# A new order for every instruction of an attention and feed-forward kernel

## The chip, the cores and the metric

One core of one Trainium2 chip runs the whole kernel in one launch. The metric is the time of that launch in device microseconds. Beside it stands a profile of one execution, with a span from the first to the last instruction.

## The reference

Attention with a window of 128 positions and 4 sink positions, then a feed-forward layer with a squared ReLU. q, k and v are 4 x 8 x 768 x 64 in fp32 (batch, heads, positions, head size).

```python
scores = scale * np.matmul(q, k.transpose(0, 1, 3, 2))
keep = is_sink | in_window            # position < 4, or 0 <= query - key < 128
a = softmax(np.where(keep, scores, -1e9))
x = np.matmul(a, v).transpose(0, 2, 1, 3).reshape(3072, 512)
h = x @ w_in                          # 512 x 2048
r = np.maximum(h, 0.0)
out = (r * r) @ w_out                 # 2048 x 512, fp32 out
```

## The kernel before

Matmuls run in bf16 with fp32 accumulation. The four batches pass through the same stages: load, transpose q and k, scores, exp, mask, values, normalize, transpose the result (`xT`), layer 1, ReLU and square (`gT_sb`), layer 2, store. A batch has 6 tiles of 128 positions, worked on in 3 pairs.

Batch 0's q and k come in fp32 by SyncE's queue and are cast ("regroup") and transposed on TensorE. All other q and k tiles, all v tiles and the weights come by DMAs that GpSimd issues, which cast to bf16. Batches 2 and 3 transpose q, k and `xT` with DMA transposes on SyncE's queue. Layer 1 of batches 0 and 1 is plain (`layer1`, L709). Layer 1 of batches 2 and 3 (`layer1_fast`, `quad`, L875) and layer 2 of all but two pairs (`layer2_fast`, L1089) form a product of 2 x 2 blocks from seven smaller products. These need sums of inputs on VectorE (`sum`, L1047: s1 to s4; `xs`), and sums of outputs (`less`, `pair_sum`, `last_quarter`, `middle`).

**What sets the order.** Every piece of work is an `Op` with a number, in the order of its creation, and with the engines that may run it. `Plan.run` walks through the string `ORDER`: the word `57p+60` emits op 57 on TensorE with 60 dummies ahead of it. The letters are p TensorE, v VectorE, a ScalarE (ACT), g GpSimd (POOL), s SyncE's queue. Each engine runs its own ops in that order, and an op waits for the data it reads. So the string decides the order on each engine and, where an op allows more than one engine, also which one runs it. Buffers are handed out in the same walk, so they follow the order too.

On GpSimd, some ops have another form than on VectorE. A mask (`mask 512`) is one multiply by a triangle on VectorE (L587) and two selects on GpSimd (L199). The in-place sums `sum either` (L1047, s3 into `gT_sb`) and `last either` (L1147) are a VectorE add or a DMA from SBUF to SBUF that GpSimd issues and that adds to its destination:

```python
if e == "pool":
    nc.gpsimd.dma_start(out=t_["x"], in_=t_["u"], accum_op=ALU.add)
    return
nc.vector.tensor_tensor(out=t_["x"], in0=t_["x"], in1=t_["u"], op=ALU.add)
```

**Dummies.** `warm` issues transposes of the identity into a tile that is overwritten afterwards. They compute nothing. The last ones of a group are 128 x 128, those ahead of them 32 x 32.

**Ops that the text names** (batch.pair in brackets):

| op | what it is |
|---|---|
| 3, 5, 4 | GpSimd builds the identity, the bias, the triangles |
| 55 k, 56 q; 67 k, 68 q; 61 k, 62 q | regroup of batch 0's head pairs 0; 2; 1 |
| 57 k, 58 q; 69 k, 70 q; 63, 64 | their transposes on TensorE |
| 59 k, 60 q; 71, 72; 65, 66 | unloads of these from PSUM to `qkT` |
| 83, 84; 85, 86 | first scores (with bias), first exps |
| 21, 24, 25, 26; 19, 20, 22, 23 | loads of the four slices of `w_in`; of v |
| 157, 163, 169, ...; 124 | layer 1 of batch 0; transpose of its second pair |
| 257; 259 | a mask of [1.2]; the values that read it |
| 680, 681; 684, 685 | s1, s3 of [2.0]; the products that read them |
| 718, 719; 723 | s1, s3 of [2.2]; the product that reads s3 |
| 830, 831; 835 | the same of [3.0] |
| 691; 693; 694 | a product of [2.0]; its pair sum; its "last either" |
| 664, 666; 672, 674 | masks of [3.2] for the values 668; for 676 |

## Time and profile before

| | |
|---|---|
| time, three runs | 209.57, 211.17, 212.15 us (median 211.17) |
| the profiled execution | 209.85 us, span 208.1 us |
| TensorE (PE) | 199.2 us busy, 96% of the span |
| VectorE (DVE) | 171.5 us, 82% |
| ScalarE (ACT) | 126.4 us, 61% |
| GpSimd (POOL) | 96.1 us, 46% |
| DMA | 26.10 MB in 93882 packets, mean 125 GB/s |

In the profile, L709 is line 709 of the kernel. A row of the waits reads: engine, tile and line that waited, who ended the wait, total in us, times, longest. A group reads: line, engine, operation, output and input with their shape, count, busy us and mean ns of one, then the idle time of the engine just before and what ended it. A piece of the chain that ended last reads: start, length, engine, tile, line, count. A stretch reads: its bounds and length, then busy us and the number of instructions of each engine that touch it, the granted TensorE clock, the mean busy share of the DMA engines, GB/s. PE's matmuls are pipelined and their ends are modelled, so short gaps do not show as idle time.

### The profile page before, as it was taken

How to read it: one execution, taken by the hardware profiler on the slowest of the kernel's cores; microseconds unless marked ns; L12 is line 12 of the kernel's file. 1: busy time of each engine (PE TensorE's matmuls, PEld its weight loads, DVE VectorE, ACT ScalarE, POOL GpSimd, SP SyncE). 2: the span in 40 equal slices, each digit the busy share in tenths (PEclk: the TensorE clock that was granted, in tenths of full speed). 3: DMA queues.
4: the chain of work that ended last, by engine and by line, in shares of the span. 5: the costliest groups of instructions: out<-in, count | busy, mean ns of one | idle time of the engine just before them, and what ended most of it. 6: DMA issues, size and time to landing. Idle time of an engine off the chain costs nothing.

```text
span 208.1 us, 5793 instructions
## 1 busy us (share of the span) xinstructions
PE 199.2 (96%) x2441; PEld 163.7 (79%) x2441; DVE 171.5 (82%) x311; ACT 126.4 (61%) x168; POOL 96.1 (46%) x133
## 2 busy tenths in 40 slices
PE   7788999999999999999999999999999999999993
PEld 6447998568557864568798799999889999999892
DVE  3478669788499782699999999999999889999853
ACT  3594034658988716798774746789964075776110
POOL 7959874399899996480490069400050000000000
PEclk9999999999999999999999999999999999999999
DMA  5999999999999999999914529980024302200025
GB/s 147 283 184 205 179 193 212 172 155 201 160 158 133 158 125 150 137 197 156 241 27 127 79 17 98 93 254 3 0 54 146 58 2 104 102 3 0 0 104 202
DMA packets 93882, 26.10 MB, mean 125 GB/s; under 512 B 86816, under 2 KB 91552, under 8 KB 93856
## 3 DMA queue, kind: packets, MB, share of 16 engines
q0 software_dynamic: 69248, 12.59, 79.1%
q1 hardware_dynamic: 24280, 12.94, 28.9%
q8 instruction: 19, 0.31, 0.7%
q10 hardware_dynamic: 328, 0.20, 0.3%
q14 instruction: 7, 0.06, 0.1%
HBM read 27.30 MB, written 6.29 MB: 161 GB/s over the span
## 4 chain that ended last, share of the span: by engine, by line
PE 73%; POOL 10%; DMA 5%; ACT 3%; DVE 3%; issue 3%; ACTq 0%; SPq 0%
PE py L1089 26%; PE pm L875 18%; PE pm L709 17%; PE po L634 4%; POOL v L343 4%; POOL qn L332 4%; PE ps L555 4%; DMA qn<-in_k_dram 4%; POOL expm L199 2%; PE py L970 2%; ACT expm L575 2%; DMA qr<-in_q_dram 2%; PE po L609 1%; PE pt L445 1%; ACT qs L180 1%
## 5 line engine op out<-in xcount | busy, mean ns | idle before, releaser
L575 ACT ACTIVATE expm<-ps 128x1024 bf16<-128x1024 f32 (+1 forms) x48 | 44.3, 955 | 5.9 <-PE ps L555 5.8
L709 PE MATMUL pm<-xT,w_in_sb 128*128 128x256 bf16 (+1 forms) x320 | 44.0, 294 | 0.4 <-ACT r L720 0.4
L199 POOL TENSOR_SCALAR_AFFINE_SELECT expm<-expm 128x512 bf16<-128x512 bf16 x32 | 24.3, 793 | 42.7 <-ACT expm L575 42.6
L709 PEld LDWEIGHTS <-w_in_sb 128*128 128x128 bf16 x320 | 34.5, 114 | 6.9 <-issue 0.6
L1089 PEld LDWEIGHTS <-gT_sb 128*128 128x128 bf16 x336 | 31.1, 98 | 3.7 <-issue 0.2
L1089 PEld LDWEIGHTS <-sg 128*128 128x128 bf16 x240 | 22.4, 98 | 3.3 <-issue 0.6
L720 ACT ACTIVATE r<-pm 128x1024 bf16<-128x1024 f32 x14 | 14.3, 1025 | 17.3 <-PE pm L709 17.1
L875 PE MATMUL pm<-xs,w_in_sb 128*128 128x128 bf16 (+1 forms) x256 | 24.0, 246 | 0.0
L343 POOL DMA_DIRECT2D v<-in_v_dram x24 | 21.4, 899 | 2.6 <-DMA qn<-in_q_dram 1.6
L875 PEld LDWEIGHTS <-w_in_sb 128*128 128x128 bf16 x256 | 22.1, 114 | 0.2
L332 POOL DMA_DIRECT2D qn<-in_q_dram x20 | 17.7, 887 | 8.8 <-DMA w_out_sb<-in_moe_w_out_dram 5.9
L897 ACT ACTIVATE gT_sb<-r 128x1024 bf16<-128x1024 bf16 x19 | 19.5, 1053 | 2.4 <-DVE r L949 2.3
L1089 PE MATMUL py<-wt,gT_sb 128*128 128x256 bf16 x160 | 20.8, 273 | 0.0
L1089 PE MATMUL py<-wt,sg 128*128 128x256 bf16 x160 | 20.6, 273 | 0.0
L332 POOL DMA_DIRECT2D qn<-in_k_dram x20 | 17.7, 890 | 2.3 <-issue 1.1
L1089 PE MATMUL py<-w_out_sb,gT_sb 128*128 128x256 bf16 x144 | 18.5, 273 | 0.0
L650 DVE TENSOR_TENSOR xn_sb<-po,rc 128x512 bf16<-128x512 f32 (+1 forms) x28 | 17.2, 615 | 1.0
L937 ACT ACTIVATE r<-pm 128x1024 bf16<-128x1024 f32 x11 | 11.2, 1024 | 10.2 <-DVE sg L1047 5.8
L722 DVE TENSOR_SCALAR r<-pm 128x1024 bf16<-128x1024 f32 x10 | 12.1, 1228 | 5.7 <-PE pm L709 5.7
L875 PEld LDWEIGHTS <-qkT 128*128 128x128 bf16 x192 | 16.1, 114 | 0.5 <-issue 0.4
L922 DVE TENSOR_TENSOR t<-t,pm 128x512 f32<-128x512 f32 x24 | 15.5, 681 | 1.0 <-ACT t L180 0.5
L949 DVE CUSTOM_DVE_ANT_1 r<-pm,t 128x1024 bf16<-128x1024 f32 x12 | 14.4, 1220 | 1.8 <-PE pm L875 1.4
(95 smaller groups left out, 324.4 us busy)
## 6 DMA issues: line engine op xcount, KB each, us to landing
out_dram<-osb SPq DMA_DIRECT2D x11, 512.0 KB, 3.9
v<-in_v_dram POOLq DMA_DIRECT2D x24, 128.0 KB, 7.8
qn<-in_k_dram POOLq DMA_DIRECT2D x20, 128.0 KB, 8.3
qn<-in_q_dram POOLq DMA_DIRECT2D x20, 128.0 KB, 7.8
w_in_sb<-in_moe_w_in_dram POOLq DMA_DIRECT2D x4, 512.0 KB, 10.8
w_out_sb<-in_moe_w_out_dram POOLq DMA_DIRECT2D x4, 512.0 KB, 11.1
qr<-in_k_dram SPq DMA_DIRECT2D x4, 256.0 KB, 5.0
qr<-in_q_dram SPq DMA_DIRECT2D x4, 256.0 KB, 6.0
```

The lines of the kernel that those rows point to most:

```text
L199: nc.gpsimd.affine_select(out=e_tile, in_=e_tile, compare_op=ALU.is_ge, fill=fill, base=i - 1, pattern=[[0, n], [1 if i else -1, 128]], ch ...
L332: nc.gpsimd.dma_start(out=qn_t[b, ti][:, t, :].rearrange("p (h d) -> p h d", d=D), in_=(q, k)[ti][b, :, 128 * t:128 * t + 128, :].rearrang ...
L343: nc.gpsimd.dma_start(out=v_sb[b % 2][:, t, :, 0:D], in_=v[b, :, 128 * t:128 * t + 128, :].rearrange("h p d -> p h d"))
L575: nc.scalar.activation(out=x[:, :, o:512], in_=bank_t["s", b, s, m][:, :, o:512], func=AF.Exp, scale=scale)
L650: touch(("po", b, s, m0), e, nc.vector.tensor_tensor(out=xn_sb[:, 2 * s:2 * s + 2, :].rearrange("p i (j q h d) -> q p j i h d", j=2, q=2, ...
L709: nc.tensor.matmul(pm[:, i, :], lhsT=w_in_sb[:, fb // 4, kb, fb % 4:512:4], rhs=xT[:, c0 // 256:(c0 + cw) // 256, kb, :], start=(kb == 0), ...
L720: nc.scalar.activation(out=o, in_=h, func=AF.Relu)
L875: touch(tag, e, nc.tensor.matmul(y[:, bk, :, i, :], lhsT=weights(name, f0 + i, a), rhs=rhs[:, a, :], start=fresh and i == 0 and a == 0, st ...
L897: nc.scalar.activation(out=d, in_=x, func=AF.Square)
L922: touch(tag, e, nc.vector.tensor_tensor(out=T["t"], in0=T["t"], in1=bank(bk), op=ALU.subtract), bk)
L949: touch(tag, e, nc.vector._custom_dve(TENSOR_ADD_SAT, out=r, in0=both(), in1=t, s0=3.4028235e38, s1=0.0), 0, 1)
L1089: ins = nc.tensor.matmul(y_, lhsT=x[:, i, :], rhs=r_, start=(first or tail and n == 2) and i == 0, stop=i == HB - 1, skip_group_check=not ...
```

## The change

The string `ORDER` is replaced as a whole, with the same 888 ops, and one constant of `warm`. Here are the lines around the ops that the text names; every other line of the string changes too.

```diff
 ORDER = """
-0v 8s 9s 1v 56a 55a 3g 7a 10s 57p+60 58p 60v 11s 5g 6g 19g 4g 20g 67v 69p+12 21g 68g 59a 12s 13s 70p+1 83p 71a 61v
-72a 14s 15s 22g 23g 84p 63p 102p 65v 85a 62a 86a 24g 25g 79g 103p 106a 73v 74v 64p 75p 76p 104a 66v 91p 113p 78v 93a
...
-635p 685p 687p 638a 636a 686v 578v 662p 626p 639v 565v 683v 637v 688p 690v 579v 561a 663a 640p 575a 689a 641v 665a
...
+0v 5g 3g 8s 9s 4g 55a 10s 11s 12s 1v 19g 13s 14s 15s 57p+47 59a 67v 7a 69p+21 56a 58p 60a 71a 68v 70p+1 61a 83p 72v
+62a 85a 84p 86a 63p 103p 102p 64p 73v 75p 20g 21g 65v 74v 6g 22g 23g 24g 25g 104a 66v 106a 91p 76p 105v 78v 87p 89p
...
+550v 574a 575a 589a 590p 591p 684p 576p 577p 611g 453g 491g 654g 592v 635p 622s 623s 457s 656g 638a 682v 686v 495s
+681g 685p 636a 551a 687p 683v 578v 624g 637v 690v 621s 639v 689v 593v 662p 626p 688p 663a 640p 691p 642s 579v
...
+675p 667p 649p 705a 737a 701v 674g 666g 668p 694g 669v 738v 650p 651v 707p 672g 709v 676p 677v 756p 742p 744a 743p
...
         for i in range(P.dummies):
-            n = 32 if P.dummies - i > 24 else 128
+            n = 32 if P.dummies - i > 18 else 128
```

What follows from the two strings:

- Dummies: 60 + 12 + 1 before, of which 36 are small; 47 + 21 + 1 after, of which 29 + 3 are small. Each group ends with its full ones: 24 before, 18 after at most.
- GpSimd starts with the bias (5) and the identity (3) comes second; before it was the other way round. A regroup (68) leaves GpSimd.
- ACT takes 55, 59, 56, 60, 71, 61, 62 ahead of the first exp (85); before, 56, 55, 59, 71, 72.
- 58p stands behind 69p and its dummies; before, it stood ahead of them.
- VectorE to GpSimd: seven "last either" (453, 472, 491, 694, 713, 732, 844) and three "sum either" (681, 719, 831), all of which are accumulating DMAs there, and 8 masks. GpSimd to VectorE: 5 masks and the regroup.
- Between ACT and VectorE: to VectorE go 6 ReLUs, 8 squares, 4 unloads and 1 strided one, 3 transposed copies, 8 copies, 4 "first_quarter", 2 "first", 1 evacuation; to ACT go 5 ReLUs, 11 squares, 5 unloads and 1 strided one, 3 transposed copies, 3 copies, 1 "first_quarter" and 1 regroup.
- TensorE has the same steps in another order; the 28 steps ahead of 157 are the same set.

More of the change, by code (lines that the diff above doesn't have):

```diff
@@ L18 @@
 ORDER = """
-0v 8s 9s 1v 56a 55a 3g 7a 10s 57p+60 58p 60v 11s 5g 6g 19g 4g 20g 67v 69p+12 21g 68g 59a 12s 13s 70p+1 83p 71a 61v
-72a 14s 15s 22g 23g 84p 63p 102p 65v 85a 62a 86a 24g 25g 79g 103p 106a 73v 74v 64p 75p 76p 104a 66v 91p 113p 78v 93a
-87p 77a 115a 89p 88v 105v 80v 90v 95p 92p 94a 26g 116g 81p 107g 96v 114p 82a 97p 119p 27g 28g 29g 30g 31g 32g 33g
-108p 98v 117a 99p 109p 100a 118v 120p 111p 122p 101v 157p 121v 112v 123v 110v 163p 124p 169p 164v 126v 16s 125v 166p
-170v 160p 161a 158v 167v 175p 176v 168v 2v 131p 133a 162a 127g 128p 178p 179v 130v 129v 132v 34g 35g 36g 37g 38g 39g
@@ L24 @@
-40g 41g 180v 172p 173a 287p 137p 145p 136p 42g 43g 44g 45g 147a 177v 148v 288p 140a 289p 134p 146p 174v 141v 138a
-139v 159v 290p 46g 47g 48g 49g 50g 291p 149a 150v 135a 151p 142p 143p 144v 152p 292p 153v 293p 154p 155v 156a 294p
-165a 295v 171a 296a 181p 272v 184p 182a 196p 199p 202p 185a 187p 205v 201v 183a 200a 204v 273v 190p 197v 274v 203a
-188a 189v 198a 216p 191a 217a 276p 277p 297s 234p 219a 51g 52g 53g 54g 353g 220v 235a 193p 194a 278p 218v 186v 195v
-206v 279p 237a 226p 229a 354g 355g 356g 357g 358g 359g 360g 361g 280p 209p 372s 275v 210a 212a 227a 192v 298v 299v
@@ L29 @@
-362g 363g 364g 365g 374s 371s 375s 373s 281p 282p 284a 221p 248p 245p 211v 213v 222v 247a 249a 283p 285a 302p 377s
-376s 366g 246v 250v 207p 367g 261p 208a 262a 238v 236v 214p 230v 215v 303p 305p 228g 304a 264a 253p 239p 300v 254a
-256a 368g 240p 241v 306p 223p 263g 369g 231p 251p 301v 370g 232p 224a 225a 252a 594g 265g 257g 595g 596g 233v 307a
-308v 309p 258p 266p 242p 597g 311v 244v 255v 310p 378s 380s 17s 243a 312v 313p 259p 267p 335p 260v 314v 315a 387p
-268v 329p 388a 330a 338p 336v 390a 339a 340v 331v 326p 394p 317p 327a 598g 599g 600g 397a 269p 318v 271a 328a 270v
@@ L34 @@
-395a 320p 411p 321a 412a 332p 333a 414a 398v 384v 391v 396v 389v 413v 322v 323p 392p 399p 324a 319a 334a 337v 393v
-400v 325v 341p 379s 403p 347p 342v 381s 612s 614s 601g 316s 382s 458v 404a 460v 459v 439v 350p 348a 406a 421p 616s
-613s 462p 424a 602g 603g 604g 605g 383g 464a 422a 463p 465p 385p 415g 351v 440v 349v 407v 461v 423g 352a 386a 466p
-416p 429p 417p 432a 405v 468v 615s 402s 617s 619s 286s 441v 430a 418v 496v 467v 469p 425g 433g 431g 344p 401s 501v
-18s 426p 408p 618s 409p 427p 471v 345a 470p 473p 428v 472v 410v 474v 504v 443p 444p 628p 346a 445a 475a 498v 505v
@@ L39 @@
-434p 446p 629a 448a 631a 442v 502v 497v 435p 447p 652p 420s 476s 449v 450p 419s 630v 436v 438s 437s 451p 500v 625v
-454p 655a 343a 477v 644p 653a 506p 647a 507p 520p 521p 508a 510p 645a 522a 481p 452v 503v 478v 453v 479v 482p 509v
-523v 499v 480v 511v 524p 484p 525v 512p 526p 513p 455v 486a 483a 514a 527p 632v 528a 485p 646g 516p 517p 530p 606g
-537v 534v 488p 456a 529a 535v 518v 536v 487v 531p 633p 580p 490v 532v 489p 491v 634v 581p 582a 492p 493v 552p 566p
-567p 583v 533a 515a 584p 553p 494v 538p 586p 539p 607g 654g 621s 620s 495s 608g 622s 457s 568a 519a 609g 623s 610g
@@ L44 @@
-611g 648v 624g 585v 680v 540a 554a 541v 587p 542p 556p 588a 555v 589a 543v 544p 557v 569v 656g 590p 545p 570p 546a
-558p 559p 591p 682v 560a 547a 571v 681v 592v 572p 548p 549p 573p 574a 593a 562p 563p 550v 551a 684p 564v 576p 577p
-635p 685p 687p 638a 636a 686v 578v 662p 626p 639v 565v 683v 637v 688p 690v 579v 561a 663a 640p 575a 689a 641v 665a
-691p 627a 692p 670p 671a 718v 657p 699v 666v 642s 693v 672g 695p 658p 673a 664g 700v 703p 694v 659v 696v 643s 704p
-705a 697a 706p 649p 675p 667p 650p 674v 701v 651v 676p 668p 737a 738v 669v 707p 742p 743p 756p 744a 746p 757p 758a
@@ L49 @@
-708a 740v 677v 760p 722p 698s 660s 741v 719v 723p 739v 702v 710p 759v 745v 761v 747v 709v 661s 748p 749p 762p 711p
-678s 763p 764a 765a 714p 725p 727a 724a 679s 750v 720v 752p 766p 753p 751a 712v 713v 721v 715v 716a 770v 726p 767p
-729p 754v 728v 768v 717s 816p 817p 730p 771v 731v 732v 774p 772v 773v 733p 769a 818a 819v 734v 775p 802p 820p 803p
-776a 777v 804a 806p 735a 805v 821v 788p 778p 822p 755a 790a 807v 823p 830v 824a 789p 808p 792p 809p 826p 827p 779v
-832v 780p 810a 812p 781p 813p 791v 831v 794p 793v 828v 795p 782a 796a 834p 797a 829a 833v 783v 835p 784p 811v 814v
@@ L54 @@
-785p 786v 798p 799p 836a 837p 736s 825a 815a 800v 838p 840v 839v 801v 841p 787a 843v 849v 842p 868v 845p 850v 853p
-854p 856p 855a 851v 857p 872p 869v 873p 870v 875p 858v 844v 846v 859v 847a 852v 860p 848s 861p 864p 862v 871v 863v
-865v 877a 874a 878v 866v 876p 879p 881v 882v 867s 880p 883p 887s 884v 886s 885v
+0v 5g 3g 8s 9s 4g 55a 10s 11s 12s 1v 19g 13s 14s 15s 57p+47 59a 67v 7a 69p+21 56a 58p 60a 71a 68v 70p+1 61a 83p 72v
+62a 85a 84p 86a 63p 103p 102p 64p 73v 75p 20g 21g 65v 74v 6g 22g 23g 24g 25g 104a 66v 106a 91p 76p 105v 78v 87p 89p
@@ new lines @@
+93a 113p 26g 79g 77a 107g 95p 92p 115a 90v 116g 80v 88v 94a 114p 96v 81p 82a 97p 27g 98v 119p 108p 99p 117a 118v
+109p 100a 101v 111p 120p 122p 28g 29g 30g 31g 32g 33g 34g 35g 123v 121v 110v 112v 157p 163p 124p 164v 126v 169p 125a
+158v 160p 166p 161a 167v 170a 175p 128p 131p 178p 129a 133a 159v 162v 176v 172p 179v 287p 130v 132v 168v 145p 173a
+36g 37g 127g 38g 39g 40g 41g 177a 165v 2v 42g 174v 180v 136p 137p 147a 140a 148v 138a 139v 141v 288p 289p 134p 290p
+146p 43g 291p 44g 45g 46g 135a 142p 149a 150v 151p 143p 152p 292p 144v 293p 153v 154p 295v 156a 47g 48g 49g 294p 50g
@@ new lines @@
+296a 51g 52g 53g 155v 184p 272v 54g 353g 181p 16s 185v 205v 199p 196p 202p 171a 182a 190p 201a 200a 187p 186v 197a
+371s 297s 198v 203v 204a 191v 273v 354g 355g 356g 188a 216p 192v 217a 274v 276p 277p 193p 194v 357g 358g 359g 360g
+361g 362g 219a 17s 195v 189a 234p 235a 237a 278p 279p 226p 280p 227a 238g 209p 220v 183v 298v 210a 218v 374s 212a
+281p 299v 228v 363g 229a 230g 372s 375s 364g 236g 221p 282p 248p 245p 283p 378s 377s 206v 300v 222v 246v 302p 211v
+247v 373s 249a 250a 284v 285a 207p 213v 208a 261p 264a 303p 304a 262a 214p 275v 305p 307a 215v 253p 254a 265g 239p
@@ new lines @@
+365g 383g 255g 366g 367g 368g 256a 240p 263v 241v 369g 306p 301v 223p 379s 376s 231p 251p 225v 232p 224a 309p 252a
+233v 370g 594g 595g 308v 258p 266p 242p 244a 310p 243v 267p 311v 257v 268v 313p 259p 335p 314v 260v 315a 387p 336a
+329p 390a 388a 394p 395a 317p 338p 397a 326p 389v 312v 391v 318v 319a 339a 330v 596g 396v 269p 597g 398v 327v 271v
+320p 411p 270a 340a 331a 321v 414a 412a 322a 328a 598g 599g 600g 384v 415v 332p 333v 612s 382s 381s 316s 392p 323p
+601g 602g 413g 603g 604g 605g 399p 324a 393v 334v 400v 341p 337a 325a 403p 380s 18s 406a 616s 402s 347p 404a 458v
@@ new lines @@
+348a 342a 460v 405v 459v 462p 350p 421p 351a 422a 424a 463p 385p 423g 425g 407g 465p 439v 461v 441v 464v 625v 466p
+386a 416p 429p 467a 614s 432a 440v 617s 613s 442v 401s 606g 607g 286s 615s 417p 469p 497v 418v 344p 408p 352a 430a
+431g 433g 426p 409p 427p 343a 345a 619s 608g 468v 471v 496v 470p 473p 443p 618s 501v 444p 428v 609g 472g 434p 474v
+410v 445v 499v 475a 349a 628p 620s 629a 446p 631a 435p 502v 498v 652p 447p 505v 450p 448v 653a 449v 436v 452v 451p
+346a 644p 655a 454p 645a 647a 520p 506p 521p 507p 508a 510p 500v 503v 477v 455v 478v 419s 479v 509v 511v 522v 438s
@@ new lines @@
+476s 437s 481p 482p 420s 484p 483v 504v 512p 513p 523v 524p 514a 487v 526p 485p 525v 480v 456v 536v 486a 630v 516p
+527p 528a 632v 517p 518v 534v 488p 530p 490v 531p 537v 532v 633p 634v 580p 489p 492p 582a 529a 538p 493v 540a 494v
+581p 539p 583v 535v 552p 553p 584p 566p 567p 542p 515a 554a 568a 555v 541v 543v 556p 558p 544p 545p 557v 559p 570p
+569v 572p 586p 585v 587p 533a 519a 546a 560a 680v 571v 562p 563p 548p 547a 588a 648v 564v 561a 549p 573p 610g 646g
+550v 574a 575a 589a 590p 591p 684p 576p 577p 611g 453g 491g 654g 592v 635p 622s 623s 457s 656g 638a 682v 686v 495s
@@ new lines @@
+681g 685p 636a 551a 687p 683v 578v 624g 637v 690v 621s 639v 689v 593v 662p 626p 688p 663a 640p 641v 691p 642s 579v
+692p 565a 665a 627a 670p 657p 658p 673a 671a 695p 693v 699v 643s 718v 703p 664v 700v 659v 704p 719g 696v 697v 706p
+675p 667p 649p 705a 737a 701v 674g 666g 668p 694g 669v 738v 650p 651v 707p 672g 709v 676p 677v 756p 742p 744a 743p
+702v 757p 746p 741v 740v 739v 745v 708a 758a 722p 723p 748p 760p 660s 759v 747v 710p 749p 762p 711p 712v 761v 763p
+764a 750a 698s 679s 714p 720v 725p 661s 766p 767p 678s 772v 724v 715v 726p 752p 753p 721v 729p 728v 768v 770v 716a
@@ new lines @@
+765a 754v 816p 774p 751v 818v 727a 775p 817p 731v 730p 733p 755a 776a 777v 819v 771v 820p 802p 734v 735v 769a 830v
+778p 803p 804a 805v 788p 790a 789p 822p 780p 821v 806p 792p 823p 713g 831g 824a 791v 807v 773v 808p 809p 794p 779v
+826p 827p 810a 825v 793v 828v 812p 781p 795p 813p 832v 796a 782a 732g 717s 834p 736s 797a 829a 811a 833v 814v 835p
+836v 798p 799p 784p 783a 785p 837p 800v 838p 786v 841p 840v 839a 801v 787v 842p 845p 815a 843v 849v 853p 868v 850v
+872p 851v 846v 869v 855a 844g 854p 856p 873p 852v 847v 857p 875p 858a 859v 870v 848s 874a 860p 861p 864p 876p 862v
@@ L57 @@
+877v 878v 863v 871v 879p 880p 865v 866a 881v 882v 867s 884v 883p 887s 886s 885v
 """
```

## Prediction

> **What bounds the kernel now.** I read the page first (two lines), then the busy time of each engine in long stretches (two rows).

> ```profile
> span 208.1 us, 5793 instructions
> PE 199.2 (96%) x2441; PEld 163.7 (79%) x2441; DVE 171.5 (82%) x311; ACT 126.4 (61%) x168; POOL 96.1 (46%) x133
> ...
> 0.00:19.10 19.10, 14.48 (x236) 10.50 (x237) 10.94 (x31) 12.65 (x18) 15.38 (x32) 1.00 1.21 205
> 19.10:203.00 183.90, 182.94 (x2189) 151.72 (x2186) 158.55 (x276) 113.74 (x150) 80.76 (x102) 1.00 1.09 115
> ```

> The columns after the length are PE, weight loads, DVE, ACT, POOL. From 19.1 us, where the first layer-1 product starts, to 203.0, PE is idle for 183.90 - 182.94 = 0.96 us. Its waits there are few (the waits of PE in that stretch, then the end of the chain of waits, then one line of the DMA issues):

> ```profile
> PE po L634 <- POOL expm L199: 0.4, 1, 0.4
> PE pm L709 <- ACT r L720: 0.4, 1, 0.4
> PE pm L875 <- ACT expm L575: 0.2, 1, 0.2
> ...
> 198.60 4.38 PE py L1089 x40
> 203.00 0.43 DVE u L1120
> 204.77 0.29 DVE half L182
> ...
> out_dram<-osb SPq DMA_DIRECT2D x1, 64.0 KB, 2.0
> ```

> Three waits, 1.0 us. The rest of the span is the front (19.1 us, PE idle for 4.6 of it and on dummies for several more) and the tail: four VectorE instructions behind the last sums, a store that lands 2.0 us after its issue. So the kernel is bound by TensorE's own work behind a front that its feeders set. A new order has the same matmuls (4 dummies fewer), so it can win only the front, 1.0 us of waits and the tail. That bound carries the forecast.

> **The front.** The 28 TensorE steps ahead of the first layer-1 product (157p) are the same set in both orders, and the layer-1 products behind it begin 157, 163, 124, 169 in both; what moves is when 157p starts. Timeline rows of the start, then one group of the identity tile, then two stretches with that tile alone:

> ```profile
> 1.15 0.29 POOL L225 TENSOR_SCALAR_AFFINE_SELECT ident<-ident 128x128 bf16<-128x128 bf16 x1 [0.63 <-DVE ident L207]
> 1.42 0.77 POOL L199 TENSOR_SCALAR_AFFINE_SELECT biases<-biases 128x256 bf16<-128x256 bf16 x2
> 1.50 3.81 PE L173 MATMUL pt<-ident 32*32 32x32 bf16 x60 [1.50 <-POOL ident L225]
> 2.92 0.30 POOL L236 MEMSET biases<- 4x256 bf16 x1
> 4.58 0.63 ACT L180 ACTIVATE qs<-qr 128x512 bf16<-128x512 f32 x1 [2.48 <-DMA qr<-in_q_dram]
> 8.56 1.08 ACT L180 ACTIVATE qkT<-pt 128x512 bf16<-128x512 bf16 x2 [1.55 <-PE pt L445]
> 9.53 0.82 ACT L575 ACTIVATE expm<-ps 128x768 bf16<-128x768 f32 x1
> 16.83 1.02 ACT L575 ACTIVATE expm<-ps 128x1024 bf16<-128x1024 f32 x1 [0.27 <-PE ps L555]
> ...
> L173 PE MATMUL pt<-ident x73: 182/219/311, 1.5 to 8.4; 128*128 128x128 bf16 x37, 32*32 32x32 bf16 x36
> ...
> 3.00:4.00 1.00, 1.00 (x12) 1.00 (x11) 0.00 (x0) 0.00 (x0) 1.00 0.97 338
> 6.45:7.05 0.60, 0.60 (x15) 0.60 (x12) 0.00 (x0) 0.00 (x0) 1.00 1.02 352
> ```

> *The identity is late.* GpSimd now builds the bias (5g) before the identity (3g), and every dummy reads the identity. The bias ends at 2.92 + 0.30 = 3.22, the identity 0.29 later, so the dummies start at about 3.6 instead of 1.50.

> *The clock.* The last two rows count dummies that touch a stretch: 12 in 1.0 us with a length of 0.31 (the largest of L173) is one each 0.107 us; 15 in 0.6 us with 0.22 (the median) is one each 0.056. So TensorE ran at half rate up to about 6.3, although the granted clock reads 1.00, which only says that nothing was recorded earlier. The 60 dummies: (3.81 - 0.31 - 24 x 0.107) / 36 = 0.026 us for a small one.

> *The new dummies.* 29 small and 18 full: 0.75 + 1.93 us, from 3.6 to 6.3, which is when 57p's four real transposes begin (about 5.8 before). With 0.43 for them and 0.2 of latency, the first unload (59a) starts at 6.9.

> *ACT's list.* 60a unloads the q transposes (58p), which now stand behind 69p with its 21 dummies: from 6.7, 3 x 0.026 + 18 x 0.056 to 0.107, then eight transposes and the latency, so 60a starts at 8.45 if the clock opens at once, at 9.75 if it does not. Then 60, 71, 61 and 62 pass ACT at 0.5 each (two unloads between 8.56 and 9.53), and the first exp starts at 10.4 to 11.8 instead of 9.53. From there to the end of the eighth exp ACT took 17.85 - 9.53 = 8.3 us, of which 0.5 was 62a, now done: 7.8, so it ends at 18.2 to 19.6 instead of 17.85, and 157p behind it moves by +0.35 to +1.75. ACT's waits for PE in that list (0.27 in the row) may shrink. I take **+0.7**.

> On the other side, an early front is stopped by the weights (a timeline row, the landing of `w_in_sb`'s four loads, a piece of the chain):

> ```profile
> 9.49 1.51 POOL L279 DMA_DIRECT2D w_in_sb<-in_moe_w_in_dram  x2
> ...
> DMA to landing us min/median/max: 9.2/10.8/11.9
> ...
> 23.13 7.11 PE pm L709 x64
> ```

> 169p reads the third slice, issued at about 10.2; it lands by 10.2 + 11.9 = 22.1 and 169p starts at 23.1. GpSimd reaches that issue at 9.9 in the new order (0.6 of regroup gone from it, nothing else ahead that was not there), so 157p gains at most about 1.3.

> [...]

> **What moves from VectorE to GpSimd.** Ten in-place sums become accumulating DMAs that GpSimd issues: seven "last either" (L1147) and three "sum either" (L1047). None ran in before. Three more masks go to GpSimd on balance. Groups by line and shape, then DMA issues (the first between 120 and 140 us, the others of the whole run):

> ```profile
> L1147 DVE TENSOR_TENSOR osb<-osb,u 128x256 f32<-128x256 f32 x10 | 5.1, 512 | 0.1
> L1047 DVE TENSOR_TENSOR gT_sb<-gT_sb 128x1024 bf16<-128x1024 bf16 x10 | 6.8, 684 | 0.0
> L199 POOL TENSOR_SCALAR_AFFINE_SELECT expm<-expm 128x512 bf16<-128x512 bf16 x32 | 24.3, 793 | 42.7 <-ACT expm L575 42.6
> L332 POOL DMA_DIRECT2D qn<-in_k_dram x20 | 17.7, 890 | 2.3 <-issue 1.1 <-DMA v<-in_v_dram 0.5 <-DMA qn<-in_q_dram 0.4
> ...
> qn<-in_k_dram POOLq DMA_DIRECT2D x2, 128.0 KB, 3.6
> ...
> qn<-in_k_dram POOLq DMA_DIRECT2D x20, 128.0 KB, 8.3
> w_out_sb<-in_moe_w_out_dram POOLq DMA_DIRECT2D x4, 512.0 KB, 11.1
> ```

> VectorE loses 7 x 0.51 + 3 x 0.68 = 5.6 us by this. That is worth nothing by itself: PE waits for VectorE nowhere after 19.1 by the rows above. What it costs is latency. An issue holds GpSimd for 0.89 us and lands after 3.6 us when the queues are quiet (loads at 122 to 126 us) and after as much as 11.1 when they are full. Which end counts is read from who waits. A "last either" is waited for by a store alone. A "sum either" feeds a matmul. I place these by PE's own work, in steps like these pieces of the chain:

> ```profile
> 143.49 0.87 PE py L1089 x8
> 144.36 0.87 PE pm L875 x8
> 145.24 0.43 PE ps L555 x8
> 149.38 0.36 PE po L634 x12
> ```

> 681g can start when 680v has read its source, about when PE is at 140; 685p needs it, and nine quad products of four matmuls (0.44 each), 684p (0.87) and a score (0.43) lie between: 5.3 us. For 719g before 723p it is about 8 us, for 831g before 835p about 9. After 100 us the load queue is thin (loads of batch 3 alone), so I take the quiet 3.6 us, or 5 for twice the bytes: **0**, with no cover left at 681g. At 11.1 the waits are 5.8, 3.1 and 2.1: **+11**.

> **One new wait that can be added up.** GpSimd's queue near 152 us reads 719g, 674g, 666g, 694g, 672g. 719g waits for the sum 718v, which stands behind 693v, which waits for the product 691p. So three masks are queued behind an accumulation. From the end of 691p: 0.2 latency, VectorE 0.4 + 2 x 0.7 = 1.8, then GpSimd 0.89 + 2 x 1.59 + 0.89 + 1.59 = 6.55: 8.5 us. On PE from there to 676p, which reads the last mask, there are six sums (5.2), scores and values: 8.0 us. **+0.5**; between 0, if VectorE runs ahead, and more by as much as it runs late.

> **Waits that go.** The longest wait after 19.1 (values 259p for a mask on GpSimd, at 75 us) goes, since that mask (257) is on VectorE again: **-0.4**; of the other 0.6 I count nothing, and all 1.0 as the bound. The tail has the same last steps: 0.

> **Sum.** +0.7 - 0.4 + 0.5 = +0.8 on the profiled execution's 209.85 us (span 208.1 and 1.75 around it): 210.65. The median shown, 211.17, is 1.32 above that execution, so I forecast **212.0**. The best end is -1.3 - 1.0 = -2.3, or 208.9.

> **Rivals.**
> *A sum that lands late* (slower). The three accumulations before matmuls land with the latency of a full queue. For it: no row shows this DMA, it reads two operands, and 681g has 5.3 us. Against: the queue is nearly empty then, and 3.6 us is measured there. It decides from 5.3 us on; at 8.3 us (the page's median for k loads) it costs 3.0 + 0.3 = 3.3, at 11.1 it costs 11: 215.3 to 223, middle 219. Chance 0.22.
> *VectorE late, and masks behind it* (slower). VectorE is busy 158.55 of the middle's 183.9 us, and two-input multiplies on it meet GpSimd's masks (timeline rows):

> ```profile
> 63.71 2.88 DVE L587 TENSOR_TENSOR expm<-expm,tri 128x1024 bf16<-128x1024 bf16 x3
> ...
> 65.38 1.70 POOL L199 TENSOR_SCALAR_AFFINE_SELECT expm<-expm 128x512 bf16<-128x512 bf16 x2
> ```

> Three multiplies take 2.88 us, and a mask beside them 1.70 against 1.59. If VectorE is 3.5 us behind near 150 us, 676p waits 4 us: 216. The 5.6 us taken off VectorE speak against it, its other moves (two "first", five copies, a relu more) give some 2 back. Chance 0.18, 0.14 of it beyond 2%.
> [...]
> *A late clock.* [...] Chance 0.12, within 2%.
> *The gains alone.* The front finds its 1.3 us and no new wait opens: 208.9. For it: ACT's 0.27 us waits and PE's 4.6 idle us in the front. Chance 0.10; 0.05 more for something the trace does not show that gains over 2%.

> **How the numbers follow.** Forecast 0.33, late clock 0.12, gains 0.10 and the milder part of the VectorE case 0.04 stay within 2%: 0.59, less 0.02 for the forecast's own upper tail, 0.57. Slower by over 2%: 0.22 + 0.14 + 0.02 = 0.38. Faster by over 2%: 0.05, because 4.2 us aren't there to be won. Two per cent is about what a measurement of this kernel can tell from no change. The likeliest case alone spans 209.0 to 214; to leave out no more than 2 in 10, the range goes from 209.0 into the late sums, to 218.0.

> **What would show it.** First dummy at about 3.6 us; full-rate dummies not before 7; first exp at 10.4 to 11.8; first L709 product at 19.5 to 20.9; PE idle from there to the end under 2 us, with a wait of some 0.5 us for GpSimd near 158; accumulations landing within 5 us. Wrong, if 157p starts before 18, if PE waits for a sum's DMA near 145, 162 or 185, or if VectorE releases PE over and over between 100 and 190.

## The result, and the profile after

The new order takes 211.19 us (median of 22 runs, 210.79 to 211.44) against 209.83 us for the order before (22 runs on the same chip, 209.45 to 212.15). The ratio is 1.0059, 95% interval 1.0047 to 1.0072: a small loss, far inside two per cent. The profiled execution took 211.43 us, with a span of 209.7. In experiments 1, 2 and 3 below, two, one and two of the twelve runs lay over 1.5% above the fastest; the ratios leave them out, the medians do not.

The page and the two long stretches of after, to be laid beside those of before (columns after the length: PE, weight loads, DVE, ACT, POOL, granted clock, DMA share, GB/s):

```profile
span 209.7 us, 5812 instructions
...
PE 199.6 (95%) x2432; PEld 164.2 (78%) x2437; DVE 167.9 (80%) x306; ACT 124.3 (59%) x161; POOL 105.6 (50%) x148
...
0.00:19.10 19.10, 14.19 (x185) 10.46 (x185) 8.91 (x27) 12.20 (x18) 14.40 (x30) 1.00 1.21 208
19.10:203.00 183.90, 182.11 (x2212) 150.87 (x2217) 156.32 (x274) 111.68 (x143) 91.19 (x119) 1.00 1.24 124
```

The work moved off VectorE (171.5 to 167.9 us) to GpSimd (96.1 to 105.6), and TensorE is as full as it was. The span grew by 1.6 us, and the timeline rows of the start show where (of before the first layer-1 product, then the rows of after):

```profile
19.14 3.11 PE L709 MATMUL pm<-xT,w_in_sb 128*128 128x256 bf16 x27
...
3.52 2.98 PE L173 MATMUL pt<-ident 32*32 32x32 bf16 x47 [3.52 <-POOL ident L225]
6.30 0.63 PE L445 MATMUL pt<-ident,qs 128*128 128x128 bf16 x4
6.86 2.29 PE L173 MATMUL pt<-ident 32*32 32x32 bf16 x21
8.94 1.06 PE L445 MATMUL pt<-ident,qs 128*128 128x128 bf16 x8
20.77 1.47 PE L709 MATMUL pm<-xT,w_in_sb 128*128 128x256 bf16 x12
...
3.88 0.63 ACT L180 ACTIVATE qs<-qr 128x512 bf16<-128x512 f32 x1 [1.78 <-DMA qr<-in_k_dram]
6.97 0.60 ACT L180 ACTIVATE qkT<-pt 128x512 bf16<-128x512 bf16 x1 [2.46 <-PE pt L445]
6.97 1.28 ACTq L363 DMA_DIRECT2D vs_in<-in_v_dram  x1
8.30 0.63 ACT L180 ACTIVATE qs<-qr 128x512 bf16<-128x512 f32 x1 [0.74 <-issue]
10.04 1.09 ACT L180 ACTIVATE qkT<-pt 128x512 bf16<-128x512 bf16 x2 [1.11 <-PE pt L445]
12.05 4.08 ACT L575 ACTIVATE expm<-ps 128x768 bf16<-128x768 f32 x5
```

The first dummy waits for the identity until 3.52. The first cast is done at 3.88 + 0.63 = 4.5, but 57p's four transposes stand behind 47 dummies and start at 6.3. ACT unloads them at 6.97, then issues the load of `vs_in` (the row of that issue runs to 8.25; ACT's idle 0.74 us fall almost wholly into it), then casts q (56a) at 8.30. TensorE's eight transposes of 69p and 58p at 8.94 still run at half rate (1.06 us; four take 0.40 at full rate, at 8.13 in before). So 60a starts at 10.04, the first exp at 12.05 (9.53 before) and the first layer-1 product at 20.77 (19.14 before): +1.63. From there to the end of the span it is 209.7 - 20.8 = 188.9 us, and 208.1 - 19.1 = 189.0 before. **In these two executions the whole difference is the front.**

Waits of PE from 20.8 us on, and the piece of the chain around the longest:

```profile
PE po L634 <- POOL expm L199: 0.6, 2, 0.3
PE pm L709 <- ACT r L720: 0.4, 1, 0.4
PE py L970 <- issue: 0.3, 2, 0.2
...
155.03 2.83 POOL expm L199 x4
157.86 0.81 POOL osb L1145
158.67 1.25 POOL expm L199 x2
159.97 0.63 PE po L634 x15
```

The chain spells out the queue that the prediction added up: masks, the accumulation 694g, the mask 672g, then 676p. The wait at 75 us is gone. In place of 1.0 us of waits there are 1.3, and the same matmuls were busy for some 0.5 us less.

The new accumulating DMAs (KB each, then the median time from issue to landing):

```profile
osb<-u POOLq DMA_DIRECT2D x7, 128.0 KB, 3.3
gT_sb<-gT_sb POOLq DMA_DIRECT2D x3, 256.0 KB, 3.9
```

### The profile page after: what moved, and what is told of

Read it like the earlier page. It is cut to its first block, busy times and chain, and to the rows that moved or that the text cites. A ratio compares the mean times of both kernels' runs of the same rounds, so it can differ in the third digit from the quotient of the medians.

```text
span 209.7 us, 5812 instructions
## 1 busy us (share of the span) xinstructions
PE 199.6 (95%) x2432; PEld 164.2 (78%) x2437; DVE 167.9 (80%) x306; ACT 124.3 (59%) x161; POOL 105.6 (50%) x148
## 4 chain that ended last, share of the span: by engine, by line
PE 82%; ACT 6%; DVE 5%; POOL 3%; issue 2%; POOLq 0%; DVEq 0%; ACTq 0%
PE py L1089 24%; PE pm L709 20%; PE pm L875 16%; PE py L970 7%; PE po L634 4%; PE ps L555 4%; ACT expm L575 3%; PE pt L173 2%; POOL expm L199 2%; ACT gT_sb L897 1%; PE px L679 1%; DVE sg L1047 1%; PE po L609 1%; ACT qkT L180 1%; PE pt L426 1%
## 5 line engine op out<-in xcount | busy, mean ns | idle before, releaser
L575 ACT ACTIVATE expm<-ps 128x1024 bf16<-128x1024 f32 (+1 forms) x48 | 43.5, 953 | 3.1 <-PE ps L555 2.9
L709 PE MATMUL pm<-xT,w_in_sb 128*128 128x256 bf16 (+1 forms) x320 | 44.4, 294 | 0.4 <-ACT r L720 0.4
L709 PEld LDWEIGHTS <-w_in_sb 128*128 128x128 bf16 x320 | 34.3, 114 | 6.8 <-issue 1.0
L199 POOL TENSOR_SCALAR_AFFINE_SELECT expm<-expm 128x512 bf16<-128x512 bf16 x38 | 26.7, 766 | 18.6 <-ACT expm L575 18.4
L1089 PEld LDWEIGHTS <-gT_sb 128*128 128x128 bf16 x336 | 30.8, 98 | 4.2 <-issue 1.0
L1089 PEld LDWEIGHTS <-sg 128*128 128x128 bf16 x240 | 22.6, 98 | 3.0 <-issue 0.4
L875 PE MATMUL pm<-xs,w_in_sb 128*128 128x128 bf16 (+1 forms) x256 | 23.6, 246 | 0.0
L343 POOL DMA_DIRECT2D v<-in_v_dram x24 | 22.3, 936 | 1.3 <-DMA qn<-in_q_dram 1.0
L875 PEld LDWEIGHTS <-w_in_sb 128*128 128x128 bf16 x256 | 22.1, 114 | 0.1
L937 ACT ACTIVATE r<-pm 128x1024 bf16<-128x1024 f32 x12 | 11.9, 1023 | 15.1 <-PE pm L875 13.4
L332 POOL DMA_DIRECT2D qn<-in_q_dram x20 | 17.8, 898 | 6.1 <-DMA w_out_sb<-in_moe_w_out_dram 4.4
L1089 PE MATMUL py<-wt,gT_sb 128*128 128x256 bf16 x160 | 20.8, 273 | 0.0
L722 DVE TENSOR_SCALAR r<-pm 128x1024 bf16<-128x1024 f32 x12 | 14.6, 1221 | 7.6 <-PE pm L709 7.6
L1089 PE MATMUL py<-wt,sg 128*128 128x256 bf16 x160 | 20.6, 273 | 0.0
L1145 POOL DMA_DIRECT2D osb<-u x7 | 6.6, 945 | 27.7 <-DVE u L1120 27.7
L897 ACT ACTIVATE gT_sb<-r 128x1024 bf16<-128x1024 bf16 x18 | 18.5, 1055 | 2.3 <-DVE r L949 2.3
L720 ACT ACTIVATE r<-pm 128x1024 bf16<-128x1024 f32 x12 | 12.1, 1023 | 11.4 <-PE pm L709 11.4
L332 POOL DMA_DIRECT2D qn<-in_k_dram x20 | 17.8, 898 | 1.5 <-issue 0.9
L1089 PE MATMUL py<-w_out_sb,gT_sb 128*128 128x256 bf16 x144 | 18.5, 273 | 0.0
L1045 POOL DMA_DIRECT2D gT_sb<-gT_sb x3 | 2.6, 868 | 28.5 <-PE pm L875 11.4
## 6 DMA issues: line engine op xcount, KB each, us to landing
out_dram<-osb SPq DMA_DIRECT2D x11, 512.0 KB, 3.1
v<-in_v_dram POOLq DMA_DIRECT2D x24, 128.0 KB, 8.1
qn<-in_k_dram POOLq DMA_DIRECT2D x20, 128.0 KB, 7.1
qn<-in_q_dram POOLq DMA_DIRECT2D x20, 128.0 KB, 7.6
w_in_sb<-in_moe_w_in_dram POOLq DMA_DIRECT2D x4, 512.0 KB, 11.2
w_out_sb<-in_moe_w_out_dram POOLq DMA_DIRECT2D x4, 512.0 KB, 10.4
```

The costliest lines, as they stand in the source:

```text
L199: nc.gpsimd.affine_select(out=e_tile, in_=e_tile, compare_op=ALU.is_ge, fill=fill, base=i - 1, pattern=[[0, n], [1 if i else -1, 128]], ch ...
L332: nc.gpsimd.dma_start(out=qn_t[b, ti][:, t, :].rearrange("p (h d) -> p h d", d=D), in_=(q, k)[ti][b, :, 128 * t:128 * t + 128, :].rearrang ...
L343: nc.gpsimd.dma_start(out=v_sb[b % 2][:, t, :, 0:D], in_=v[b, :, 128 * t:128 * t + 128, :].rearrange("h p d -> p h d"))
L575: nc.scalar.activation(out=x[:, :, o:512], in_=bank_t["s", b, s, m][:, :, o:512], func=AF.Exp, scale=scale)
L709: nc.tensor.matmul(pm[:, i, :], lhsT=w_in_sb[:, fb // 4, kb, fb % 4:512:4], rhs=xT[:, c0 // 256:(c0 + cw) // 256, kb, :], start=(kb == 0), ...
L722: nc.vector.tensor_scalar_max(o, h, 0.0)
```

## The experiments

Ratios are to the order before, run beside each kernel on the same chip, with their 95% intervals. All edits are to the order of after, unless said otherwise.

**1. The identity first.**
```
-0v 5g 3g 8s 9s
+0v 3g 5g 8s 9s
```

> Edit: in the order of after, the identity (3g) is built ahead of the bias (5g); nothing else moves. Theory (the late identity makes the front): first dummy at about 1.5 us instead of 3.52; its 47 dummies (2.7 us) end before the first cast (55a, 3.88 to 4.5), so 57p's transposes start at 4.5 to 4.6 instead of 6.30; the full rate comes near 6.3; the unload of the q transposes (60a) starts at 7.6 to 8.2 instead of 10.04 and the first L709 product at 18.3 to 19.0 instead of 20.77. Time 208.7 to 209.6, 1.6 to 2.5 under after. Rival (ACT's casts and the queued loads set the front, not the identity): the first L709 product moves by less than 0.5 us, time 210.7 to 211.3.

Measured: 210.64 us, ratio 1.0028 (1.0000 to 1.0056). Its timeline:

```profile
1.50 2.98 PE L173 MATMUL pt<-ident 32*32 32x32 bf16 x47 [1.50 <-POOL ident L225]
7.23 1.04 PE L445 MATMUL pt<-ident,qs 128*128 128x128 bf16 x8
19.35 2.89 PE L709 MATMUL pm<-xT,w_in_sb 128*128 128x256 bf16 x25
```

The late identity is worth 1.42 us of the front's 1.63 in this pair of profiles. The place of the first product moves from execution to execution (20.12 to 20.78 in five with the front of after, 19.35 here and 19.41 in experiment 12, which has this front), so 0.7 to 1.4 is what these rows support. The ratios give 0.31%, some 0.65 us; this kernel's runs spread from 209.75 to 212.13. The expectation was too hopeful by 0.4 us at the first product, and the time is 1 us above its range: TensorE ran from 1.50 on and its transposes at 7.23 were still at half rate (1.04 us for eight). The full rate did not come at 6.3 as in before.

**2. No dummies ahead of 57p.**
```
-57p+47
+57p
```

> Edit: in the order of after, the 47 dummies ahead of the first transposes (57p) are left out; the 21 ahead of the q transposes stay. Theory A (the dummies stand in the way: 57p waits for their end, 1.9 us behind its data): 57p at 4.6, the first unload at 5.0, ACT's second cast at about 6.4, 60a at 8.2 instead of 10.04, and what the later clock takes back is under 1 us: time 209.6 to 210.4. [...]

Measured: 210.11 us, ratio 1.0004 (0.9978 to 1.0030). Timeline:

```profile
4.32 0.61 PE L445 MATMUL pt<-ident,qs 128*128 128x128 bf16 x4 [4.32 <-ACT qs L180]
6.98 1.03 PE L445 MATMUL pt<-ident,qs 128*128 128x128 bf16 x8
19.15 3.11 PE L709 MATMUL pm<-xT,w_in_sb 128*128 128x256 bf16 x27
```

Theory A holds: with the identity as late as ever, 57p starts 2.0 us earlier and the first layer-1 product 1.6 us, although the transposes at 6.98 run at half rate. The 47 dummies cost more by standing in TensorE's queue than the clock gives for them.

**3. The front of before, the rest of after** (60 and 12 dummies with the sizes of before, its engines and its order up to 157p).

> Edit: the order of before up to the first layer-1 product (157p) with its engines and its 60 and 12 dummies, then the remaining operations in the order of after. Theory (all of the +1.6 us is the front; the body behind it is worth -0.05): first L709 product at about 19.1 as in before, time within 0.5 of before: 209.4 to 210.2. Rival (the bodies differ too, in what the front hands on: six steps of GpSimd and VectorE that after puts ahead of 157p come behind it here): a wait opens behind 157p, 210.5 to 211.5.

Measured: 210.52 us, ratio 1.0030 (1.0003 to 1.0058), between the two expectations.

```profile
18.85 3.66 PE L709 MATMUL pm<-xT,w_in_sb 128*128 128x256 bf16 x32
64.78 0.29 PE L516 MATMUL pk<-qkT,kblk 128*32 128x256 bf16 x4 [0.46 <-DVE qkT L182]
```

The front is early, and the joint of the two orders costs a wait of 0.46 us for VectorE at 64.8. That does not account for all of it; the body took 208.8 - 18.85 = 189.9 us, 1.0 more than in either kernel.

**4. Before, with the bias ahead of the identity.**
```
-... 58p 60v 11s 5g 6g ...     (3g stands after 55a)
+... 55a 5g 3g ...
```

> Edit: in the order of before, the bias (5g) is built ahead of the identity (3g); nothing else moves. Theory (the late identity alone makes the front): first dummy at about 3.55 instead of 1.50, the 60 dummies end near 7.4, 57p and 58p at half rate to about 8.3, and the first L709 product at 20.6 to 21.0 instead of 19.14: time 211.2 to 211.8. Rival (the weights' landing and ACT's list hide it): under 0.6 us, time 209.8 to 210.4.

Measured: 210.49 us, ratio 1.0030 (1.0008 to 1.0051): +0.6 us, just above the rival's range and under the theory's. The one trace is of the longest of the twelve executions, 212.64 us. In it the first exp starts at 10.90, 1.37 us after that of before, so the late identity delays this front too; why the other executions lose only some 0.6 us, no trace shows. The first layer-1 product comes at 21.48, later than expected, and these stretches show why (columns as above):

```profile
15.78:19.19 3.41, 2.21 (x36) 0.99 (x33) 2.97 (x10) 3.14 (x5) 2.13 (x4) 1.00 1.29 205
19.19:22.60 3.41, 3.41 (x54) 3.01 (x55) 2.73 (x9) 0.64 (x2) 3.41 (x5) 0.50 1.27 204
```

The granted clock falls to 0.50 for 3.41 us, after 3.41 us in which TensorE was busy for 2.21; the last steps ahead of the first layer-1 product run at half rate.

**5. An earlier front and no wait for the masks.**
```
-0v 5g 3g 8s 9s 4g 55a ... 7a 69p+21 ... 719g ... 694g
+0v 3g 5g 8s 9s 4g 7a 55a ... 69p+10 ... 719v ... 694v
```

> Edit, on the order of after: the identity (3g) ahead of the bias (5g); the load of vs_in on ACT's queue (7a) ahead of the first cast, where ACT waits for data anyway; 10 dummies instead of 21 ahead of the q transposes; the sums 719 and 694 on VectorE again. Theory (the front is ACT's list behind 57p and 58p, and the wait near 158 us is the masks queued behind the two accumulations): 57p at 4.3, second cast at 5.5, 60a at about 7.2 (10.04 in after, 8.56 in before), first L709 product at 18.2 to 18.7 (20.77, 19.14), and PE's wait for GpSimd's masks at po (0.6 us in after) gone. Time 208.3 to 209.3, under both. Rival (the landing of the weights holds the layer-1 products, or the full rate comes later because TensorE has less to do in the front): first L709 product at 18.2 to 18.7, but the time comes back as waits of PE for w_in or as half-rate products: 209.5 to 210.5.

Measured: 210.58 us, ratio 1.0035 (1.0011 to 1.0059). Nearest to the rival, though the first product is later than both had it. Stretches:

```profile
5.41:8.83 3.42, 1.78 (x23) 1.12 (x23) 1.46 (x3) 2.15 (x5) 3.35 (x7) 1.00 1.24 331
8.83:12.24 3.41, 3.41 (x31) 1.63 (x31) 2.11 (x4) 2.54 (x5) 3.28 (x6) 0.50 1.64 211
```

60a came at 7.40 as hoped, but TensorE, with 11 dummies fewer, was busy for only 1.78 us of one stretch and got half rate in the next, and the first product came at 19.31. The wait for the masks went; waits for VectorE of 0.3, 0.2 and 0.2 us took its place.

**6. All ten sums back on VectorE** (453, 472, 491, 694, 713, 732, 844, 681, 719, 831: g to v).

> Edit, on the order of after: the ten sums that became accumulating DMAs are on VectorE again; the three extra masks stay on GpSimd. Theory (the accumulations cost only the wait of the masks queued behind two of them, and win nothing since PE does not wait for VectorE): PE's wait for GpSimd at po goes from 0.6 us to under 0.2 and no other wait opens: 210.4 to 210.9, 0.3 to 0.8 under after. Rival (VectorE needs the 5.6 us that they take off it): waits of PE for VectorE open between 100 and 200 us and the time is 211.5 to 214.

Measured: 217.64 us, ratio 1.0375 (1.0333 to 1.0417). My theory falls by 7 us; the rival's waits are there, and the time is above its range too. Waits of PE from 21 us on, then a piece of the chain:

```profile
PE py L1089 <- DVE gT_sb L1047: 2.4, 1, 2.4
PE pm L875 <- DVE xs L832: 1.3, 1, 1.3
PE pm L875 <- DVE t L922: 0.8, 1, 0.8
...
146.75 3.02 DMA out_dram<-osb
```

Near 125 us PE waits 2.1 us for VectorE. None of the ten sums holds VectorE there: another sum took 3.34 us instead of 0.68, beside four selects of GpSimd (rows in the last section). In after, these selects stand on GpSimd behind the accumulation 491, which waits for VectorE, and start at 131.65; with it gone they ran at 121.61. Near 146 the sums 453 and 491, at the places that suit GpSimd, come late on VectorE; the store behind them frees the osb buffer at 149.8, VectorE waits for it, and the product that reads 681 waits 2.4 us. The granted clock is 0.50 for the 3.4 us behind that. This run also tells about the front of after, which it shares:

```profile
6.87 1.42 PE L173 MATMUL pt<-ident 32*32 32x32 bf16 x21
8.99 0.40 PE L445 MATMUL pt<-ident,qs 128*128 128x128 bf16 x4 [0.47 <-ACT qs L180]
```

Here the 21 dummies took 1.42 us instead of 2.29, so the full rate came among them. Even so 58p waited for ACT's cast and started at 8.99, and 60a at 9.43.

**7. Eight more sums on GpSimd** (299, 312, 440, 459, 478, 700, 850, 863: v to g).

> Edit, on the order of after: the other eight sums that may be accumulating DMAs become ones too (299, 440, 459, 478, 700 and 850 feed matmuls; 312 and 863 a store). Theory (what decides is the time from the issue to the consumer against a landing of 3 to 5 us): the sum at 194.3 us and the one at 154.0 are read by matmuls some 1.5 us later, so PE waits for their DMAs by 2 to 3 us each; the one at 120.5 by about 1; the one at 98.9 by up to 1; one more issue ahead of the masks near 155 adds 0.9 to the wait there. The others are covered. In all +5 to +9: 216 to 220. Rival (the landing is hidden everywhere, since TensorE runs behind VectorE): no wait for a sum's DMA over 0.5 us, 210.8 to 212.

Measured: 224.78 us, ratio 1.0698 (1.0651 to 1.0744). Waits of PE from 21 us on; DMA issues; two stretches:

```profile
PE py L1089 <- DMA gT_sb<-gT_sb: 10.0, 5, 2.6
...
gT_sb<-gT_sb POOLq DMA_DIRECT2D x9, 256.0 KB, 4.1
...
126.22:129.64 3.42, 0.86 (x8) 0.52 (x6) 2.75 (x6) 0.00 (x0) 2.89 (x4) 1.00 1.52 133
129.64:133.05 3.41, 3.39 (x16) 2.41 (x17) 0.00 (x0) 0.00 (x0) 0.00 (x0) 0.50 2.43 135
```

The cover decides: five of the six new sums that feed matmuls are waited for, 10.0 us in all at a median landing of 4.1. The first was issued at 61.58, right behind the loads of later batches, and took longest to land, 7.5 us. The time is above what I expected. The waits at 69, 105 and 130 us are 2.1, 1.8 and 2.6, where I had nothing, up to 1 and about 1; and I had left out that a stretch with such a wait can be followed by 3.4 us at half rate (granted clock 0.50 from 129.64 to 133.05).

**8. No dummies at all** (57p, 69p, 70p).

> Edit, on the order of after: no dummies at all (57p, 69p and 70p without theirs). Theory (the front is ACT's list; the clock matters only through the real matmuls that run at half rate): 57p at 4.3, 58p at 7.0, 60a at 7.9 to 8.2, the full rate not before 9 and perhaps only after 12 us, first L709 product within 0.7 us of the 19.15 that the kernel without the 47 has; time 209.8 to 211.0. Rival (the dummies are needed for the clock): the full rate comes after 15 us, the first L709 product at 20.5 or later or at half rate: 211.5 to 214.

Measured: 210.32 us, ratio 1.0019 (1.0003 to 1.0035). Timeline:

```profile
20.09 2.13 PE L709 MATMUL pm<-xT,w_in_sb 128*128 128x256 bf16 x18
```

The first product comes 0.94 us after that of experiment 2 (a little more than expected) and 0.68 before that of after. It is not ACT's list that held 58p here: 69p ahead of it waited until 8.29 for VectorE's cast of a load. With its identity so late, this order would be better without its 69 dummies; its ten runs lie between 209.79 and 210.78.

**9. The front as early as the order allows.**
```
-0v 5g 3g 8s 9s 4g 55a ... 57p+47 59a 67v 7a 69p+21 56a 58p 60a 71a 68v 70p+1
+0v 3g 5g 8s 9s 4g 7a 55a ... 57p+47 59a 67v 56a 58p+8 60a 69p+10 71a 68v 70p+10
```

> Edit, on the order of after: the identity ahead of the bias, vs_in's load (7a) ahead of the first cast, the q transposes (58p) ahead of the second k transposes (69p), and the dummies spread as 47, 8, 10 and 10 ahead of 57p, 58p, 69p and 70p so that TensorE has work from 1.5 us on; the body behind is that of after. Theory (the front is ACT's list, and the half-rate window from 8.8 to 12.2 us in the run with 10 dummies came because TensorE was busy for only 1.8 of the 3.4 us before it): no half-rate window after the full rate has come, 60a at 6.7 to 7.3 (10.04 in after), first exp at 9.0 to 9.6, first L709 product at 18.2 to 18.8, time 208.6 to 209.5, under both. Rival (the loads of q and k, not the order, set the front from there): first L709 product at 19.1 to 19.4 as in the other early fronts, 209.5 to 210.3.

Measured: 210.27 us, ratio 1.0026 (1.0005 to 1.0047). Timeline, then the chain:

```profile
18.52 3.66 PE L709 MATMUL pm<-xT,w_in_sb 128*128 128x256 bf16 x32
78.18 0.51 PE L555 MATMUL ps<-qkT 64*128 64x256 bf16 x8 [1.73 <-DMA qkT<-qn]
...
72.51 5.63 DMA qkT<-qn
```

The front did what the theory said (18.52, full rate kept) and the time did not follow. The transposing loads that TensorE needs at 78 us are issued from 59.76 on, against 61.05 in after: only 1.29 us earlier. TensorE meets the last of them and gives back 1.73 of the 2.25 us. This is one execution, of 211.08 us; what the others lost is not shown.

**10 and 11. The ten sums in two parts.** In 10, the three for matmuls (681, 719, 831) are back on VectorE; in 11, the seven for stores.

> Edit, on the order of after: only the three sums that feed matmuls (681, 719, 831) are on VectorE again. Theory (the 6.5 us of the run with all ten came from the seven sums for stores: two of them stand in VectorE's queue near 146 us, the store behind them frees the osb buffer at 149.8, and the next steps wait for it): PE waits for VectorE under 0.8 us in all, the first wait for the masks near 158 goes, 210.4 to 211.3. Rival (the three alone load VectorE too much): the wait of 2.4 us at the product that reads 681 is there, 213 to 215.

> Edit, on the order of after: only the seven sums for stores (453, 472, 491, 694, 713, 732, 844) are on VectorE again; the three that feed matmuls stay with GpSimd. Theory (as in the run before): PE's waits for t and xs near 125 us (2.1 us) are there, VectorE waits for the store at 149.9, what it does behind that comes late by 1 to 3 us: 213 to 217. Rival (the three sums for matmuls made it): no wait over 0.5 us, 210.4 to 211.5.

Measured: 10 takes 211.82 us, ratio 1.0091 (1.0077 to 1.0105); 11 takes 218.50 us, ratio 1.0392 (1.0348 to 1.0435). The timeline of 10, then the longest wait of PE in 11:

```profile
146.33 1.05 PE L1089 MATMUL py<-wt,gT_sb 128*128 128x256 bf16 x8 [0.84 <-DVE gT_sb L1047]
```

```profile
PE ps L555 <- DMA qkT<-qn: 2.7, 1, 2.7
```

The seven make it, as the theory had it; both came out 0.5 to 1.5 us dearer than expected. In 10 the waits for the masks go and 0.84 + 0.30 us of waits for VectorE come. In 11 the 2.1 us near 125 are those of experiment 6, with the same cause (a sum of 3.33 us beside four selects). The 2.7 us for a transposing load near 154 I had not foreseen: its issue stands on SyncE's queue behind the stores of the two late sums, at 149.35 instead of 135.25. After each of the two places the granted clock was 0.50 for one stretch of 3.41 us.

**12. The masks ahead of the two accumulations.**
```
-0v 5g 3g ... 704p 719g 696v ... 674g 666g 668p 694g ... 672g
+0v 3g 5g ... 704p 696v ... 674g 666g 719g 668p ... 672g 694g
```

> Edit, on the order of after: the identity ahead of the bias, and in GpSimd's queue near 155 us the accumulating DMAs 719 and 694 behind the masks 674, 666 and 672 that they stood ahead of. Theory (the wait of PE for the masks, 0.34 and 0.28 us, is the two accumulations in front of them, and nothing needs these two sooner): both waits go, no wait for a sum's DMA opens, first L709 product at 19.0 to 19.7, and from there to the end of the span 188.3 to 188.6 us instead of 189.0: 209.0 to 210.2, 0.6 us under the kernel that has only the identity moved. Rival (the masks wait for their exps, or the later accumulations are waited for): the waits stay or a wait for gT_sb's DMA opens, 210.0 to 211.5.

Measured: 209.38 us, ratio 0.9980 (0.9960 to 0.9999). Waits of PE from 19.5 us on:

```profile
PE pm L709 <- ACT r L720: 0.4, 1, 0.4
PE py L970 <- issue: 0.3, 2, 0.2
PE py L1089 <- DVE gT_sb L1047: 0.2, 1, 0.2
```

The wait for the masks is gone, no wait for a sum's DMA opened, and from the first product (19.41) to the end it is 207.7 - 19.4 = 188.3 us, as expected. This version is ahead of both orders, by 0.2% of the one before, with an interval that just leaves out no change.

## Why the prediction was right, and where it was not

**What bounds the kernel: right.** A body that TensorE fills, and a front. The body changed by -0.03 us against a predicted -0.4 + 0.5 = +0.1.

**The wait at 676p: right.** Predicted +0.5 from the queue of 719g, 674g, 666g, 694g and 672g; measured 0.34 + 0.28 = 0.62, by that chain, though the first part falls already on 668p, which reads 666g's mask. Experiment 12 takes it away by moving the two accumulations and nothing else near it.

**The wait at 75 us: right**, it went.

**The accumulations' landing, taken at 0: right.** They landed in 3.3 and 3.9 us (medians; 5.0 at most) and nobody waited. The criterion was right too, as experiment 7 shows: where the cover is short, the same DMA costs up to 2.6 us, and behind many loads it landed after 7.5.

**"Worth nothing by itself": wrong.** I read that PE waited for VectorE nowhere after 19.1 us and took the 5.6 us of sums off VectorE to be worth nothing. That row was of the order before, where these sums stand elsewhere. At the places that the new order gives them, they are not free on VectorE: by the ratios of experiments 6, 11 and 10 against 1.0059, the ten cost 3.2% (6.6 us) on VectorE, the seven whose only reader is a store 3.3%, the other three 0.3%. The seven cost more than VectorE's time. Two of them, late near 146 us, hold back a store, and with it an osb buffer and a transposing load; and one that no longer waits on GpSimd lets four selects run beside a sum near 121 us, which is the wait near 125. Each of the two places where experiment 11 waits was followed by 3.41 us at a granted clock of 0.50. So at these places the order depends on the accumulations. The rival "VectorE late, and masks behind it" had the neighbourhood (near 150 us) and the size about right, but it happens only without them, and by another path.

**The front: the mis-sized term.** I took +0.7 out of +0.35 to +1.75; it was +1.63. In the profiled execution the full rate came only by 10.3 (four transposes at 9.90 still took 0.56 us), 60a started at 10.04 behind half-rate dummies, and the first exp at 12.05, after the 10.4 to 11.8 that I gave. That is nearly the late end of my range, +1.75, and the rival "a late clock", to which I gave a chance of 0.12. The step that failed is "60a starts at 8.45 if the clock opens at once": it counted TensorE's queue and left out ACT's. 58p needs q's cast (56a), and 56a stands on ACT behind 59a and the issue of `vs_in`'s load, at 8.3. Even in the execution of experiment 6 where the dummies got the full rate, 60a started at 9.43. In the four other executions that share after's front the first product started at 20.12 to 20.78, so its cost was +1.0 to +1.6 and the low end should have been +1.0. The rest hangs on the clock: the two executions in which the 21 dummies took 2.29 us are the two latest (20.77 and 20.78).

What sets the moment of the full rate is not shown: one front in five executions had first products 0.66 us apart (20.12 to 20.78). Nor does a run show the 7 in "full-rate dummies not before 7". In after, the single dummy at 9.80 still took 0.31 us, against 0.22 at full rate (8.36 in before); in experiment 6 the full rate came among the dummies that ran from 6.87 to 8.29.

**The number.** 212.0 was forecast and 211.19 came. The sum on the profiled basis was 210.65, 0.5 low by the front; to it I added 1.32 because the median of three runs was that far above the profiled execution. The median of 22 runs of before is 209.83, at the profiled execution's 209.85, so that offset was not there. Two errors of opposite sign; that 212.0 came within 0.4% is in part luck.

Still open: the same matmuls were busy for 184.1 us from the first layer-1 product on in after and 184.6 in before, and experiment 3 lost 0.5 us in a way that no wait shows. And an earlier front gives back only part of the loss in most of these kernels: experiments 1, 3, 5 and 9, with first products at 18.52 to 19.35, stay at 1.0026 to 1.0035. I did not find what makes this.

## What to carry to other kernels

Follow a start-up through every engine's queue: behind the dummies, the second transposes here met a cast that stands on ACT behind an unload and a DMA issue (experiment 6), and without dummies the cast of a load on VectorE (experiment 8). Judge work that moves to another engine at its new place in the order: "nobody waits for this engine now" is a statement about the old places, and what stood behind the work on its new engine moves too when it goes. And price a wait of TensorE above its length where it leaves a stretch thin: here 3.41 us at a granted clock of 0.50 followed a stretch in which TensorE was busy for 0.86 of 3.42 us (experiment 7).

## What the chip showed that I had not expected

**Transposes alone raised the clock.** In after, TensorE ran nothing but dummies and real transposes, all in transpose mode, up to the first scores at 10.3, and the two bias products ahead of the first scores took 0.49 us there; at half rate, in experiment 8, they took 0.85.

**A VectorE sum beside masks.** The sum 299 took 1.89 us instead of 0.68 (timeline rows of after, VectorE and GpSimd; then the same of experiment 6, the sum behind the waits near 125 us):

```profile
60.44 1.89 DVE L1047 TENSOR_TENSOR gT_sb<-gT_sb 128x1024 bf16<-128x1024 bf16 x1
60.47 1.31 POOL L199 TENSOR_SCALAR_AFFINE_SELECT expm<-expm 128x512 bf16<-128x512 bf16 x2
...
121.22 3.34 DVE L1047 TENSOR_TENSOR sg<-sg,gT_sb 128x1024 bf16<-128x1024 bf16 x1
121.61 2.40 POOL L199 TENSOR_SCALAR_AFFINE_SELECT expm<-expm 128x512 bf16<-128x512 bf16 x4
```

The sum at 121.22 took 0.68 us in after (121.52) and in experiment 10 (120.89), where no select ran beside it.
